# Transposes two to a bank, a second job's places sooner, and branch hints in a two-layer expert kernel

## The chip, the cores and the metric

The kernel runs on one core of one Trainium2 chip. The metric is the device time of one execution in microseconds (us); the median of three runs of the kernel before is 590.13 us (589.78 to 592.05). Profiles come from one further execution, recorded by the hardware profiler.

## The reference

Three parts follow one another, all in float32:

```
x = retention(q, k, v, lam)              # 2 x 8 heads x 768 x 64, blocks of 64 -> x: 1536 x 512
logits = x @ w_gate; noisy = logits + log1p(exp(x @ w_noise)) * noise
top2 of 8 experts per token, softmax over the two
x[token] = sum over its two experts of weight * relu(x @ w1[e]) @ w2[e]     # 512 -> 1024 -> 512
logits = x @ w_gate2; e = argmax; weight = softmax(logits)[e]
out[token] = weight * relu(x @ u1[e]) @ u2[e], for the first 384 tokens of each expert, else 0
```

## The kernel before, in words

**Matmuls.** Each float32 operand is split into two float32r parts, a high one and the rest, and a product is made of three matmuls (`three`, L954 to L956; where both parts of the tokens fit into one bank of 512 columns, two matmuls, `weighted`, L1016 and L1017). TensorE (PE) only writes to PSUM, which has eight banks; the kernel names them `hp` and `tr` (two each) and `yp0` to `yp3`.

**Jobs.** The tokens of one expert, or a part of them, are a `Job`: it gathers its rows from DRAM by an indirect DMA on GpSimd (POOL; L552), adds the two rows of each token in the second layer (`both`, L563), transposes them into columns (`split_rows`: PE transposes at L941, ScalarE (ACT) casts the high part out of the bank at L943, VectorE (DVE) subtracts it to get the rest at L946), runs the first and second product of its expert, scales and scatters its rows (`finish`, L1204 and L1206, `scatter`, L1213). A job of one tile of tokens (`by_token`) makes its hidden rows first (`first_rows`, L1064) and turns them (`turn`: transposes L1072, cast L1075, subtraction L1076). The last job of all (`ends`) writes its output in halves.

The first layer has nine jobs: 288 tokens chosen early, 128 tokens (B), and seven of 408 down to 364 tokens. The second layer has jobS (256 tokens of the fullest expert, as far as known early), jobT (up to 128 more tokens of the same expert), and seven of 336, 128, 324, 128, 164, 152 and 128 tokens. `experts` walks through the steps of each job, and inside them fetches weights (SyncE, SP, L91 and L94), converts them (`convert`, ACT L109; `convert_low`, DVE L115), prepares the next job and finishes the last one; `extra1` and `extra2` put the routing between the steps.

**Places.** `one_hot` works out for a small job which tokens it has. It multiplies a marked matrix with columns of numbers (PE, L404), copies the resulting lines from PSUM to one buffer `tabi` (DVE, L406), transposes them by PE (L409) into `a` (DVE, L410), and sums. A first call reads the token numbers; `rest` reads the others: whether the place is taken, and the weight's three parts. From these come the destinations of the scatter (`dst`, L426 and L427) and the weights (`wt`, L428). jobS calls `rest` at its successor's first step, jobT at its own second step; `finish` of jobS stands in jobT's second step, that of jobT in the step after jobT.

**Leftovers.** Tokens beyond the fixed sizes are counted, and two `tc.If(total > 0)` blocks (L1567 after layer one, L1702 after the sixth job of layer two) hold a loop for them. With these inputs the total is zero and each engine takes the branch past the block. Each engine loads the total into a register (L1294), compares and branches.

**Order.** The order of instructions on each engine is made at build time by a list scheduler: by readiness in a cost model, and earlier program text first. `tc.issue_after(ins)` keeps what is traced in its block behind `ins` on that engine's queue. Each engine then works through its queue in order, waiting at an instruction until its semaphores are there.

## Time and profile before

| | us |
|---|---|
| median of 3 runs | 590.13 |
| lowest, highest | 589.78, 592.05 |
| the profiled execution's own time | 594.88 |
| its span, first to last instruction | 593.3 |
| busy: PE, PE weight loads, DVE, ACT, POOL | 580.3, 551.6, 378.6, 278.2, 173.0 |

Matmuls are pipelined and the profile models their ends, so that PE is busy for 98% of the span does not say that it runs at its peak; gaps between the starts of its matmuls, and its waits, say more. Attention fills about the first 75 us, layer one goes to about 396 us, layer two from there.

### The profile page before, as it was taken

The page shows a single profiled execution, that of the slowest core. Times are in us where ns is not written, and L with a number is a line of the kernel's source. Part 1 is how long each engine was busy: PE and PEld are TensorE (multiplying, and loading weights), DVE is VectorE, ACT ScalarE, POOL GpSimd, SP SyncE. Part 2 cuts the span into 40 slices and gives each one's busy share as a digit, 9 for nine tenths or more (in the row PEclk, how much of TensorE's full clock was granted, in tenths as well). Part 3 has the DMA queues.
Part 4 walks back from the last instruction along what each step waited for, and adds up shares of the span by engine and source line. Part 5 has one row for each costly group of instructions (what it writes and reads, how often), then busy time and mean ns, then how long its engine had stood idle before and what let it go on. Part 6 is the DMA issues. An engine that isn't in the chain of part 4 may idle for free. (4 is left out here: it accounts for less than half of the span.)

```text
span 593.3 us, 11528 instructions
## 1 busy us (share of the span) xinstructions
PE 580.3 (98%) x4269; PEld 551.6 (93%) x4269; DVE 378.6 (64%) x878; ACT 278.2 (47%) x496; POOL 173.0 (29%) x244
## 2 busy tenths in 40 slices
PE   8999999999999999999999999999989999999996
PEld 7988899989999999999999999988879999998996
DVE  6579689865364543644645545656877667667893
ACT  4666440454353433533535334244137367467782
POOL 4966300505030040120400502023275136141304
PEclk9999999999999999999999999999999999999999
DMA  9999616349444286385443512461588967966740
GB/s 183 228 281 260 200 38 195 96 153 344 135 162 145 89 269 196 117 265 155 165 166 108 194 56 58 149 218 56 175 274 294 324 194 245 324 196 219 260 147 35
DMA packets 104483, 109.26 MB, mean 184 GB/s; under 512 B 35457, under 2 KB 80513, under 8 KB 104418
## 3 DMA queue, kind: packets, MB, share of 16 engines
q1 hardware_dynamic: 96722, 83.05, 46.4%
q0 software_dynamic: 7696, 25.39, 12.3%
q8 instruction: 35, 0.57, 0.4%
q14 instruction: 30, 0.25, 0.1%
HBM read 91.39 MB, written 18.18 MB: 185 GB/s over the span
## 5 line engine op out<-in xcount | busy, mean ns | idle before, releaser
L115 DVE TENSOR_TENSOR wl<-wst,wh 128x1024 fp32r<-128x1024 f32 x107 | 135.2, 1272 | 51.6 <-ACT wh L109 46.7
L109 ACT CAST wh<-wst 128x1024 fp32r<-128x1024 f32 x107 | 111.6, 1049 | 34.4 <-PE yp L955 26.5
L954 PE MATMUL hp<-x,wh 128*128 128x364 f32 (+9 forms) x352 | 115.9, 330 | 1.0 <-PEq L1567 1.0
L955 PE MATMUL hp<-x,wh 128*128 128x364 f32 (+9 forms) x352 | 115.6, 329 | 0.0
L956 PE MATMUL hp<-x,wl 128*128 128x364 f32 (+9 forms) x352 | 114.7, 326 | 0.0
L1043 ACT ACTIVATE h<-hp 128x364 fp32r<-128x364 f32 (+9 forms) x88 | 41.1, 467 | 154.3 <-PE hp L956 140.0
L954 PE MATMUL yp<-h,wh 128*128 128x364 f32 (+8 forms) x320 | 106.4, 333 | 0.0
L956 PE MATMUL yp<-h,wl 128*128 128x364 f32 (+8 forms) x320 | 105.9, 331 | 0.0
L955 PE MATMUL yp<-h,wh 128*128 128x364 f32 (+8 forms) x320 | 105.4, 329 | 0.0
L1044 DVE SCALAR_TENSOR_TENSOR h<-hp,h 128x364 fp32r<-128x364 f32 (+9 forms) x88 | 46.2, 525 | 60.7 <-ACT h L1043 50.1
L1213 POOL DMA_INDIRECT x<-y,Rdst x22 | 21.9, 995 | 182.0 <-DVE y L1187 179.6
L954 PEld LDWEIGHTS hp<-x,wh 128*128 128x128 f32 x352 | 66.1, 188 | 2.0 <-ACTq L1567 1.3
L955 PEld LDWEIGHTS hp<-x,wh 128*128 128x128 f32 x352 | 66.1, 188 | 0.5
L956 PEld LDWEIGHTS hp<-x,wl 128*128 128x128 f32 x352 | 66.1, 188 | 0.0
L955 PEld LDWEIGHTS yp<-h,wh 128*128 128x128 f32 x320 | 60.3, 188 | 0.5 <-issue 0.2
L956 PEld LDWEIGHTS yp<-h,wl 128*128 128x128 f32 x320 | 60.3, 188 | 0.0
L954 PEld LDWEIGHTS yp<-h,wh 128*128 128x128 f32 x320 | 60.1, 188 | 0.0
L946 DVE TENSOR_TENSOR x<-tr,x 128x128 fp32r<-128x128 f32 (+9 forms) x68 | 27.3, 430 | 22.6 <-ACT x L943 22.1
L943 ACT CAST x<-tr 128x128 fp32r<-128x128 f32 (+9 forms) x68 | 24.3, 383 | 34.9 <-PE tr L941 34.2
L563 POOL TENSOR_TENSOR xg<-xg 128x512 f32<-128x512 f32 (+1 forms) x16 | 23.5, 1473 | 38.5 <-DMA xg<-x,Tsrc 24.4
L115 DVE TENSOR_TENSOR wl<-more,wh 128x1024 fp32r<-128x1024 f32 x21 | 28.2, 1357 | 3.5 <-ACT wh L109 3.5
L552 POOL DMA_INDIRECT xg<-x,Rsrc x22 | 24.4, 1110 | 18.2 <-DVE x L946 11.8
(410 smaller groups left out, 1043.2 us busy)
## 6 DMA issues: line engine op xcount, KB each, us to landing
wst<-in_moe_w_dram SPq DMA_DIRECT2D x107, 512.0 KB
more<-in_moe_w_dram SPq DMA_DIRECT2D x21, 512.0 KB
ldk<-in_k_dram SPq DMA_DIRECT2D x12, 256.0 KB
ldv<-in_v_dram SPq DMA_DIRECT2D x12, 256.0 KB
out_dram<-zero SPq DMA_DIRECT2D x12, 256.0 KB
x<-xr SPq DMA_DIRECT2D x11, 256.0 KB
ldq<-in_q_dram SPq DMA_DIRECT2D x5, 512.0 KB
ldq<-in_q_dram SPq DMA_DIRECT2D x2, 256.0 KB
```

What stands on the lines that cost most here:

```text
L109: tail["cast"] = nc.scalar.copy(hi, st).ins
L115: tail["low"] = nc.vector.tensor_sub(lo, st, hi.bitcast(F32)).ins
L552: i = nc.gpsimd.indirect_dma_start(out=r, out_offset=None, in_=x, in_offset=bass.IndirectOffsetOnAxis(ap=src(s)[:m], axis=0))
L563: tail["both"] = nc.gpsimd.tensor_add(a, a, b).ins
L943: a = nc.scalar.copy(hi[:, d, :c], ps[:, :c])
L946: v_ = nc.vector.tensor_sub(lo[:, d, :c], ps[:, :c], hi[:, d, :c].bitcast(F32))
L954: nc.tensor.matmul(ps, a[0], b[0], start=start, stop=False)
L955: nc.tensor.matmul(ps, a[0], b[1], start=False, stop=False)
L956: tail["pe"] = nc.tensor.matmul(ps, a[1], b[0], start=False, stop=stop).ins
L1043: tail["act"] = nc.scalar.activation(hh, ps, AF.Relu).ins
L1044: tail["dve"] = nc.vector.scalar_tensor_tensor(hl, ps, 0.0, hh.bitcast(F32), op0=OP.max, op1=OP.subtract).ins
L1213: i = nc.gpsimd.indirect_dma_start(out=target, out_offset=bass.IndirectOffsetOnAxis(ap=dst, axis=0), in_=y, in_offset=None, bounds_check=t ...
```

## The change

Three things change.

**Transposes.** `split_rows` took a bank for each of the four column blocks of 128 and cast and subtracted each by itself. Now, where the tokens (rounded up to whole tiles) are at most 256, a bank takes two column blocks side by side, 256 columns each, and one cast and one subtraction handle both. This holds for eight jobs: B of layer one, and of layer two jobS, jobT, and those of 128, 128, 164, 152 and 128 tokens. Others keep one block to a bank.

**Places.** `rest` can be given a list `held`: then it leaves out the computation of `dst` (the lines up to L427, moved as they are into `places`) and appends it to the list as a function, and computes `wt` directly. jobS and jobT are both called so at step 0 of jobT, one behind the other, with the other seven jobs' weights (`later[1][7]()`) between. `finish` runs the held function first, behind the last subtraction of `turn` (`tail["h"]`) on DVE.

**Hints.** `likely` marks a branch hint for all five engines, behind the last traced instruction of each: for the first `If` at step 7 of layer one's last job, for the second at step 1 of the job of layer two ahead of it.

```diff
-        def rest(tag=tag):
+        def rest(tag=tag, held=None):
+            def places():
...
             if not whole:
                 columns(2, 6, False, tag)
...
+            if held is None:
+                places()
             else:
+                held.append(places)
             nc.vector.tensor_reduce(wt[:rows_, :nt], a[:, :, 3:6], axis=AX.X, op=OP.add)
...
     def split_rows(g, n, rows_, at=None):
...
-        for d in range(DC):
-            ps = bank("tr", [P, 512])
-            for s, m in enumerate(whole_tiles(whole, rows_)):
-                nc.tensor.transpose(ps[:, s * rows_:s * rows_ + m], g[s][:m, d * w:d * w + P], ident[:m, :m])
-            c = min(n, whole)
-            a = nc.scalar.copy(hi[:, d, :c], ps[:, :c])
+        c, k = min(n, whole), 2 if whole <= 256 else 1
+        for d in range(0, DC, k):
+            ps = bank("tr", [P, k, 512 // k])
+            for i in range(k):
+                for s, m in enumerate(whole_tiles(whole, rows_)):
+                    nc.tensor.transpose(ps[:, i, s * rows_:s * rows_ + m],
+                                        g[s][:m, (d + i) * w:(d + i) * w + P], ident[:m, :m])
+            a = nc.scalar.copy(hi[:, d:d + k, :c], ps[:, :, :c])
...
-            v_ = nc.vector.tensor_sub(lo[:, d, :c], ps[:, :c], hi[:, d, :c].bitcast(F32))
+            v_ = nc.vector.tensor_sub(lo[:, d:d + k, :c], ps[:, :, :c], hi[:, d:d + k, :c].bitcast(F32))
...
         def finish(self):
...
+            for f in self.held:
+                with tc.issue_after(tail["h"]):
+                    f()
...
+    def likely(label):
+        with ExitStack() as order:
+            for x in ("pe", "act", "dve", "pool", "sp"):
+                order.enter_context(tc.issue_after(tail[x]))
+            tc.mark_branch_hint_location(label, "LikelyTaken", ENGINES)
...
     def extra1(j, i):
...
+            if i == 7:
+                likely("over1")
...
-    with tc.If(total > 0):
+    with tc.If(total > 0, label="over1"):
...
     def extra2(j, i):
+        if j == BEFORE + 1 and i == 1:
+            likely("over2")
...
         if j == 1 and i == 0:
             with tc.issue_after(tail["pe"]):
-                jobS.rest()
+                jobS.rest(held=jobS.held)
                 later[1][7]()
+                jobT.rest(held=jobT.held)
             places.append(more[2])
         if j == 1 and i == 1:
-            with tc.issue_after(tail["pe"]):
-                jobT.rest()
...
-    with tc.If(total > 0):
+    with tc.If(total > 0, label="over2"):
```

## Rows read from the trace of the kernel before

**Rows 1.** Page, part 1: busy us (share of the span) and instructions.
```profile
PE 580.3 (98%) x4269; PEld 551.6 (93%) x4269; DVE 378.6 (64%) x878; ACT 278.2 (47%) x496; POOL 173.0 (29%) x244
```
**Rows 2.** Waits of PE, whole span: us in total, times, longest.
```profile
PE yp L409 <- DVE tabi L406: 1.5, 1, 1.5
PE yp L1109 <- ACT y L1206: 0.6, 1, 0.6
```
**Rows 3.** Timeline 436.9 to 446: start, us, instruction [idle before <-releaser].
```profile
437.16 0.83 PE L404 MATMUL yp<-ohs,aux 128*4 128x128 bf16 x12
437.82 1.17 DVE L427 TENSOR_TENSOR Sdst<-Stok,Sfar 128x2 int32<-128x2 f32 x1
437.87 0.69 ACT L1206 ACTIVATE y<-yp,Swt 128x512 f32<-128x512 f32 x1 [1.37 <-DVE Swt L428]
438.61 0.50 PE L1109 MATMUL yp<-wh,h 128*128 128x512 f32 x1 [0.61 <-ACT y L1206]
439.00 0.67 DVE L1076 TENSOR_TENSOR h<-tr,h 128x512 fp32r<-128x512 f32 x1
440.25 0.27 DVE L406 COPY tabi<-yp 4x128 f32<-4x128 f32 x1
440.58 0.22 PE L409 MATMUL yp<-iw,tabi 4*128 4x4 f32 x1 [1.47 <-DVE tabi L406]
440.73 0.50 PE L1109 MATMUL yp<-wl,h 128*128 128x512 f32 x1
442.00 1.01 PE L1072 MATMUL tr<-iw,hr 128*128 128x128 f32 x4
445.36 0.79 PE L941 MATMUL tr<-iw,xg 128*128 128x128 f32 x6
```
**Rows 4.** Windows: us, busy of PE, PEld, DVE, ACT, POOL, granted clock, DMA share, GB/s.
```profile
442.00:445.40 3.40, 3.40 (x12) 2.71 (x11) 0.69 (x1) 0.59 (x1) 0.70 (x1) 0.51 0.97 311
396.00:398.00 2.00, 0.99 (x7) 0.72 (x6) 1.30 (x5) 1.80 (x3) 0.11 (x1) 1.00 0.07 22
```
**Rows 5.** Timeline 430 to 437, some instructions of PE, DVE, ACT and POOL.
```profile
431.33 1.22 DVE L115 TENSOR_TENSOR wl<-wst,wh 128x1024 fp32r<-128x1024 f32 x1
431.49 1.47 PE L404 MATMUL tr<-oh,aux 128*4 128x256 bf16 x12
433.32 0.41 DVE L406 COPY tabi<-tr 4x256 f32<-4x256 f32 x1
433.98 2.63 DVE L115 TENSOR_TENSOR wl<-wst,wh 128x1024 fp32r<-128x1024 f32 x1 [0.25 <-ACT wh L109]
433.99 0.28 PE L409 MATMUL tr<-iw,tabi 4*128 4x4 f32 x2
435.82 3.15 POOL L563 TENSOR_TENSOR xg<-xg 128x512 f32<-128x512 f32 x2 [0.30 <-DMA xg<-x,Tsrc]
435.91 0.59 ACT L1075 CAST h<-tr 128x512 fp32r<-128x512 f32 x1 [1.96 <-PE tr L1072]
436.54 0.15 DVE L410 COPY Soa<-tr 128x8 f32<-128x8 f32 x1
```
**Rows 6.** PE's queue at the two branches (source views; ns min/median/max), and PE's timeline.
```profile
L1567 PEldq COMPARE_BRANCH  x1: 1580/1580/1580, 395.8 to 395.8; - x1
L1702 PEldq COMPARE_BRANCH  x1: 345/345/345, 537.0 to 537.0; - x1
396.36 0.33 PE L956 MATMUL yp<-h,wl 128*128 128x364 f32 x1
397.70 0.36 PE L954 MATMUL hp<-x,wh 128*128 128x256 f32 x1 [1.01 <-PEq L1567]
```
**Rows 7.** A wait over the whole span, and jobT's splitting and first matmul.
```profile
PEld tr L941 <- DVE x L946: 2.8, 12, 0.3
426.75 0.47 DVE L946 TENSOR_TENSOR x<-tr,x 128x128 fp32r<-128x128 f32 x2
428.55 0.28 PE L954 MATMUL hp<-wh,x 128*128 128x256 f32 x1
```

## The prediction

> **What bounds the kernel now.** I read the page's busy times first: PE is busy 98% of the span, every other engine far less [rows 1]. So only what makes PE wait, run slower or do more can move the end. The list of PE's waits comes next: outside the attention part and the first branch the largest is 1.5 us, for DVE's copy into `tabi`, and beside it 0.6 us for ACT's scaling of jobS's output [rows 2]. Both stand in one place of the timeline, jobT's second step [rows 3], which I read line by line, with the granted clock behind it [rows 4] and the six us before it [rows 5]. Last come the two branches [rows 6] and the splitting of a small job [rows 7]. Nowhere behind jobT does the list of PE's waits name a weight transfer, and the chain that ended last is nearly all PE; I take it that time saved at 440 us is kept to the end.

> The stall, as the reader should see it in [rows 3]: at 437.16 PE takes up jobT's twelve column matmuls (L404, 0.83). At 437.99 it wants to begin jobT's second product (L1109), whose bank `yp0` ACT has yet to empty: ACT starts at 437.87, having waited 1.37 for jobS's weights (`Swt`), and PE goes on at 438.61. After one L1109 stands the transpose L409 of jobT's line in PE's queue. Its line is copied by DVE's L406 at 440.25, because DVE has L427 (1.17), L1076 (0.67) and the scaling of jobS's second tile ahead of it. PE waits 1.47 to 440.58. [...]

> **Part by part, against the profiled execution (span 593.3, own time 594.88, 4.75 above the median of 590.13).**

> *Places sooner.* From 437.16 to 445.36, where the next job's transposes start, are 8.20 us. The work in them at full clock: the columns 0.83; L409, 440.58 to 440.73, 0.15; six L1109, of which five took 440.73 to 442.00, 1.27, so 1.5; four transposes L1072, 0.4 (an estimate from the 1.01 that they take, pipelined, at half the clock); six further matmuls of the same 512 columns, 1.5. Together 4.38. So 3.82 is lost: 0.62 + 1.72 as idle time around the one L1109 (437.99 to 438.61, and about 438.86 to 440.58), and the other 1.5 by the clock [rows 3, 4].

> After the change jobT's columns and transpose stand a step earlier, behind jobS's columns at 431.49 to 432.96 [rows 5]. They still cost PE 0.83 + 0.15, now there, so the end of the step moves from 437.16 to 438.14. ACT's L1206 no longer waits for `Swt` behind L426 and L427: jobS's line is in `a` at 436.69 (L410) and the weights are summed next, with one small instruction between, by about 437.1. ACT's L1075, moved by 0.98 with the matmuls ahead of its transposes, ends at 437.48, L1206 at 438.17. PE waits 0.03 and then has L1109, L1072 and the six others in one piece: 438.17 + 1.5 + 0.4 + 1.5 = 441.57 in place of 445.36: **3.8 us less**. It holds the return of the full clock: the idle time of 1.01 us at the first branch left the granted clock at 1.00 [rows 4, 6], and no idle time as long remains here. If the clock falls all the same, 1.5 of the 3.8 are not won.

> What the step adds is a new wait, of jobT's transpose for its line in the new place. jobT's copy needs the buffer that jobS's transposes read until about 434.2 (L409, 433.99), and in that moment DVE starts a weight subtraction, L115, which takes 2.63 in place of 1.22 [rows 5]. Queued behind the waiting transpose on PE is all of the step's second half. Two ends. If the copy goes ahead of L115, it is done by 434.6 and PE has jobT's columns and other matmuls to do until then: no wait. L115 then ends some 0.7 later, at 437.3, and L1076 at about 438.1, in time for the fifth L1109. If it goes behind L115, it is done at about 437.0 (436.54 + 0.15 + 0.27), while the scheduler, reckoning L115 at about its ordinary 1.22, has put the transpose some 1.4 us too early: PE waits up to 1.4 and the gain is 2.4. I take no wait: the copy is earlier in program text than the conversion, and DVE idled 0.25 just ahead of that L115. The held L426 and L427 of both jobs then stand behind L1076, and only the scaling of jobS's second tile (which PE does not want) and scatters come after them; I cost them at nothing, and at 1.2 for L427 if that cover were gone.

> The slow L115 lies beside POOL's additions L563 (435.82 to 438.97) [rows 5]. [...]

> *Transposes.* PE's transposes are as many as before. ACT and DVE lose two instructions each in eight jobs, on engines that do not set the end: nothing. At best the waits of PE's weight loads for a free bank go, 2.8 us in twelve over the whole span, the longest 0.3 [rows 7]; eight jobs of these could give some 1 us, but they overlap with running matmuls. At worst the first block of a job comes later by one more subtraction, about 0.25 (half of 0.47). Cover: in jobT two blocks are subtracted by 427.22, 1.33 us ahead of the first matmul at 428.55 [rows 7]; if that were gone, 8 x 0.25 = 2.0. I take 0, ends -1 and +2.0.

> *Hints.* On PE the first branch took 1.58, the second 0.345 [rows 6]. With the first like the second, the branch would be over at 396.15, before PE's last matmul ends (396.36 + 0.33), and of the 1.01 idle most would go. But DVE and ACT continue as before, and the routing behind them feeds PE again, so a lead of PE alone is partly spent waiting. Ends 0 and 1.0; I take 0.3. The second branch has nothing to give. The hints themselves, one per engine and branch, I cost at nothing behind PE's queue; at the other end each spoils the fetch of the code that follows, 1.58 - 0.345 = 1.24 each time.

> The sum: 3.8 + 0.3 = 4.1 less, a span near 589.2 in the profile, and **590.13 - 4.1 = 586.0** in the plain runs.

> **Rivals.**

> *The line behind the weights.* The transpose waits up to 1.4 as worked out: 2.4 + 0.3 = 2.7, **587.4**. For it: L115 starts in the very moment in which jobS's transposes end. Against it: DVE's idle 0.25.

> *Slower: the stall moves and grows.* If jobT's transpose is queued on PE right behind its columns, at about 433.8 (432.96 + 0.83), while the copy comes behind L115 at 437.0, PE idles 3.2 instead of 2.3. Then the clock falls again, and what now runs from 432.96 to 437.16, 4.2 us of matmuls, comes behind the wait: 437.0 + 4.2 + 1.7 (half of 3.4 us at half clock) + 3.4 for the rest is 446.3 against 445.36. With no gain at the branch: **591.0**. It decides if the transpose stands more than about 2.5 us ahead of the copy's end. Against it: for jobS the scheduler left 1.0 us of other matmuls between the columns and their transpose, 432.96 to 433.99 [rows 5].

> *The hints cost a fetch.* Code ahead of a branch or behind it is fetched too late because the hinted block took its place: twice 1.24, so 586.3 + 2.5 = **588.8**, without the branch's 0.3. Against it: nothing in these rows shows a hint. [...]

> *The plain runs have less of the stall.* The profiled execution is 4.75 above their median; part of the stall and the fall of the clock may belong to that. Then some 1 us of 4.1 is won: **589.1**.

> **How the numbers follow.** The forecast 0.50, the line behind the weights 0.17, the slower one 0.08, the fetch 0.10, the plain runs 0.15. About 0.5% (3 us: below 587.2 or above 593.1) can be told from no change. The forecast's own range is 584.5 to 587.2 (clock kept, branch 0 to 1.0, transposes to -1). Faster takes 0.47 of its 0.50, 0.09 of the second and 0.04 of the last two: 0.60. Slower by 3 us needs the slower rival together with the transposes' +2.0 or the fetch: 0.04. Same: 0.36. The range 584.3 to 590.4 leaves out the slower rival and little at either end.

> **What would show it.** Right: the columns of jobT (L404, twelve) directly behind jobS's and no PE wait for `tabi`; L1109 six in a row; a granted clock of 1.00 from 430 to 455; casts of 128x256 and 128x512 in `split_rows` at no new wait of PE; PE's first branch nearer 0.35. Wrong: a wait of over 1 us of PE for `tabi` at 434 to 437, a granted clock below 1 there, or gaps of PE at the starts of the small jobs.

## The result, and the profile after

The kernel after takes 596.18 us (median of 6 runs, 594.53 to 597.73) against 591.31 of the kernel before measured beside it (589.78 to 592.47): a ratio of 1.0085, 95% interval 1.0068 to 1.0102, slower by some 5 us. Measured once more, in a later group of runs (E12 below), it was 1.0060 (1.0041 to 1.0078). The prediction was 586.0 with a range of 584.3 to 590.4, and gave "slower" 0.04.

The profiled execution of the kernel after took 597.44, its span is 595.8. The lines of the kernel after are some ten higher than those of before (`three` is L963 to L965, the columns L405, `tabi` L407, jobs' output scaling L1219, the branches L1588 and L1724). PE's waits behind 380 us, which answer to [rows 2] (us in total, times, longest; PEq is PE's sequencer):

```profile
PE yp L964 <- PEq L1588: 2.4, 1, 2.4
PE yp L963 <- ACT h L1053: 2.3, 1, 2.3
PE tr L410 <- DVE tabi L407: 0.5, 1, 0.5
PE yp L965 <- PEq L1724: 0.3, 1, 0.3
```

The wait of 1.5 for `tabi` has become 0.5, and the 0.6 for `yp` is gone. In their place stand two larger ones: 2.4 at the first branch (1.01 before, [rows 6]) and a new one of 2.3 for ACT's `h`. The stretch that answers to [rows 3] (timeline: start, us, instruction, idle time before it and its releaser):

```profile
436.30 0.83 PE L405 MATMUL yp<-ohs,aux 128*4 128x128 bf16 x12
437.94 0.28 PE L410 MATMUL tr<-iw,tabi 4*128 4x4 f32 x2 [0.49 <-DVE tabi L407]
438.79 0.22 PE L410 MATMUL yp<-iw,tabi 4*128 4x4 f32 x1
440.59 0.50 PE L1119 MATMUL yp<-wh,h 128*128 128x512 f32 x1
440.93 0.40 PE L1119 MATMUL yp<-wl,h 128*128 128x512 f32 x1
441.17 0.39 PE L1119 MATMUL yp<-wh,h 128*128 128x512 f32 x1
441.40 0.40 PE L1119 MATMUL yp<-wl,h 128*128 128x512 f32 x1
441.64 0.62 PE L1119 MATMUL yp<-wh,h 128*128 128x512 f32 x2
442.10 0.60 PE L1082 MATMUL tr<-iw,hr 128*128 128x128 f32 x4
```

This is what the first step of the prediction said: jobT's columns and transpose stand a step earlier, and the six matmuls L1119 run without a gap. The wait of 0.49 is for jobS's line. DVE's copies of both lines, at 437.48 and 438.19, come behind a weight subtraction that takes 2.30, beside POOL's addition:

```profile
435.20 1.27 POOL L570 TENSOR_TENSOR xg<-xg 128x512 f32<-128x512 f32 x1
435.26 2.30 DVE L116 TENSOR_TENSOR wl<-wst,wh 128x1024 fp32r<-128x1024 f32 x1
437.48 0.41 DVE L407 COPY tabi<-tr 4x256 f32<-4x256 f32 x1
```

So the order is that of the rival "the line behind the weights", at 0.49 in place of up to 1.4. The loss comes a few us later. ACT's timeline there, and PE's:

```profile
446.91 2.00 ACT L110 CAST wh<-wst 128x1024 fp32r<-128x1024 f32 x2
453.11 0.69 ACT L1219 ACTIVATE y<-yp,Dwt 128x512 f32<-128x512 f32 x1 [4.20 <-issue]
453.70 0.44 ACT L1053 ACTIVATE h<-hp 128x336 fp32r<-128x336 f32 x1
```

```profile
451.58 0.32 PE L965 MATMUL hp<-x,wl 128*128 128x336 f32 x1
454.19 0.42 PE L963 MATMUL yp<-h,wh 128*128 128x336 f32 x1 [2.30 <-ACT h L1053]
```

ACT stands still for 4.20 us ahead of jobT's output scaling, and "issue" says that nothing which the profile shows held it back. Queued behind it is the `h` that PE wants for the next job, of 336 tokens. PE runs out of work for 2.30 us and then, from 455.2 to 458.6, runs at a granted clock of 0.50. The windows, which answer to [rows 4] (us, busy of PE, PEld, DVE, ACT, POOL, granted clock, DMA share, GB/s):

```profile
442.00:445.40 3.40, 3.40 (x22) 2.72 (x20) 1.41 (x5) 1.37 (x3) 1.81 (x2) 1.00 0.98 315
455.20:458.60 3.40, 3.40 (x14) 3.40 (x13) 3.40 (x4) 3.05 (x4) 2.86 (x3) 0.50 0.83 309
```

At 442 the granted clock is now 1.00, and the same 3.4 us at half clock (0.51 before, 0.50 here) have moved to 455. The branches (source views; ns min/median/max), and PE's timeline at the first, answer to [rows 6]:

```profile
L1588 PEldq COMPARE_BRANCH  x1: 4152/4152/4152, 394.3 to 394.3; - x1
L1724 PEldq COMPARE_BRANCH  x1: 363/363/363, 538.8 to 538.8; - x1
396.03 0.33 PE L963 MATMUL yp<-h,wh 128*128 128x364 f32 x1
398.77 0.40 PE L964 MATMUL yp<-h,wh 128*128 128x364 f32 x1 [2.41 <-PEq L1588]
```

PE's first branch did not fall from 1.58 towards 0.35, it rose to 4.15. The two profiles add up: the 3.82 of the stall gone less 0.49 that is left of it, 1.40 more at the branch (2.41 less 1.01), 2.30 behind ACT's stop and 1.7 for the 3.4 us at half clock, together +2.1 of the 2.5 by which the spans differ. That the plain runs differ by 5 is a second matter: the profiled execution of before lies 3.6 above the median of the six runs beside it, that of the kernel after 1.3 above its own (see E11 and E15).

### The profile page after: what moved, and what is told of

The parts are those of the page before. It is cut to its first block, busy times and chain, and to the rows that moved or that the text cites. A ratio compares the mean times of both kernels' runs of the same rounds, so it can differ in the third digit from the quotient of the medians.

```text
span 595.8 us, 11507 instructions
## 1 busy us (share of the span) xinstructions
PE 580.4 (97%) x4269; PEld 553.0 (93%) x4269; DVE 374.2 (63%) x862; ACT 276.2 (46%) x480; POOL 174.5 (29%) x244
## 5 line engine op out<-in xcount | busy, mean ns | idle before, releaser
L116 DVE TENSOR_TENSOR wl<-wst,wh 128x1024 fp32r<-128x1024 f32 x107 | 132.1, 1243 | 53.4 <-ACT wh L110 50.8
L963 PE MATMUL hp<-x,wh 128*128 128x364 f32 (+9 forms) x352 | 115.9, 330 | 0.0
L965 PE MATMUL hp<-x,wl 128*128 128x364 f32 (+9 forms) x352 | 114.9, 327 | 0.0
L963 PE MATMUL yp<-h,wh 128*128 128x364 f32 (+8 forms) x320 | 106.8, 334 | 2.3 <-ACT h L1053 2.3
L965 PE MATMUL yp<-h,wl 128*128 128x364 f32 (+8 forms) x320 | 106.1, 332 | 0.0
L963 PEld LDWEIGHTS hp<-x,wh 128*128 128x128 f32 x352 | 66.4, 189 | 0.7 <-issue 0.2
L965 PEld LDWEIGHTS hp<-x,wl 128*128 128x128 f32 x352 | 66.3, 188 | 0.0
L963 PEld LDWEIGHTS yp<-h,wh 128*128 128x128 f32 x320 | 60.4, 189 | 2.6 <-ACT h L1053 2.6
L965 PEld LDWEIGHTS yp<-h,wl 128*128 128x128 f32 x320 | 60.6, 189 | 0.0
L955 DVE TENSOR_TENSOR x<-tr,x 128x384 fp32r<-128x384 f32 (+9 forms) x52 | 25.1, 515 | 22.1 <-ACT x L952 22.0
L570 POOL TENSOR_TENSOR xg<-xg 128x512 f32<-128x512 f32 (+1 forms) x16 | 26.1, 1635 | 40.1 <-DMA xg<-x,Tsrc 26.8
L952 ACT CAST x<-tr 128x384 fp32r<-128x384 f32 (+9 forms) x52 | 22.0, 452 | 32.2 <-PE tr L950 31.7
L116 DVE TENSOR_TENSOR wl<-more,wh 128x1024 fp32r<-128x1024 f32 x21 | 29.4, 1410 | 3.5 <-ACT wh L110 3.5
L559 POOL DMA_INDIRECT xg<-x,Rsrc x22 | 26.1, 1188 | 18.2 <-DVE yT L516 11.8
```

Of the source, the lines that this page charges most:

```text
L116: tail["low"] = nc.vector.tensor_sub(lo, st, hi.bitcast(F32)).ins
L559: i = nc.gpsimd.indirect_dma_start(out=r, out_offset=None, in_=x, in_offset=bass.IndirectOffsetOnAxis(ap=src(s)[:m], axis=0))
L570: tail["both"] = nc.gpsimd.tensor_add(a, a, b).ins
L952: a = nc.scalar.copy(hi[:, d:d + k, :c], ps[:, :, :c])
L955: v_ = nc.vector.tensor_sub(lo[:, d:d + k, :c], ps[:, :, :c], hi[:, d:d + k, :c].bitcast(F32))
L963: nc.tensor.matmul(ps, a[0], b[0], start=start, stop=False)
```

## The experiments

Each ratio is to the kernel before, run beside it in the same group of runs on the same chip, with its 95% interval. Before took 590.6 in the group of E1 to E4, 594.2 in that of E5 to E8, 590.4 in that of E9 to E12 and 590.8 in that of E13 to E16; why the second is slower is not known, and the record gives the same chip number for it as for the last. "Branch" is the time of PE's first branch. "Packets" counts the 8 KB packets of instruction code in the DMA view of queue q14 (30 packets, 0.25 MB on the pages of before and after; q8 has 35 of 16 KB, 0.57 MB), from 5 us before to 6 us behind POOL's first branch. No view names the engine that a packet is for; the author took those of q8 for PE's and those of q14 for the other engines'. "Stop" is ACT's idle time ahead of jobT's scaling (L1219; L1206 in before).

| | kernel | ratio | branch, us | packets | stop, us |
|---|---|---|---|---|---|
| | before, its three profiles | | 1.58, 1.96, 2.16 | 2, 2, 2 | none |
| | after | 1.0085 (1.0068 to 1.0102) | 4.15 | 1 | 4.2 |
| E1 | no hints | 0.9990 (0.9973 to 1.0008) | 4.36 | 2 | none |
| E2 | no pairs | 0.9987 (0.9972 to 1.0003) | 2.17 | 2 | none |
| E3 | old places | 1.0053 (1.0034 to 1.0072) | 3.71 | 1 | 2.7 |
| E4 | code padded behind the branch | 1.0066 (1.0049 to 1.0084) | 3.73 | 1 | elsewhere |
| E5 | hints, not ACT's | 0.9972 (0.9948 to 0.9995) | 4.64 | 2 | none |
| E6 | ACT's hints alone | 1.0065 (1.0043 to 1.0087) | 3.78 | 1 | 3.6 |
| E7 | places alone | 0.9965 (0.9941 to 0.9990) | 1.80 | 2 | none |
| E8 | no hints, last job single | 0.9969 (0.9944 to 0.9994) | 1.76 | 2 | none |
| E9 | six ACT instructions ahead | 1.0039 (1.0018 to 1.0059) | 4.30 | 2 | none |
| E10 | first hints sooner | 1.0084 (1.0058 to 1.0111) | 3.53 | 1 | 3.2 |
| E11 | before again | 1.0005 (0.9989 to 1.0022) | 1.96 | 2 | none |
| E12 | after again | 1.0060 (1.0041 to 1.0078) | 3.23 | 1 | 3.5 |
| E13 | ACT's second hint alone left | 0.9999 (0.9989 to 1.0009) | 3.65 | 2 | none |
| E14 | ACT's first hint alone left | 1.0055 (1.0040 to 1.0071) | 4.29 | 1 | 4.4 |
| E15 | before a third time | 0.9993 (0.9978 to 1.0009) | 2.16 | 2 | none |
| E16 | E8 once more | 0.9982 (0.9966 to 0.9997) | 2.74 | 2 | none |

**E1, no hints.**

```diff
-            if i == 7:
-                likely("over1")
-        if j == BEFORE + 1 and i == 1:
-            likely("over2")
```

> The kernel after without its two branch hints, all else kept. Theory A (code): ACT's 4.2 us gap ahead of the output scaling of job T and PE's long first branch (4.15 us) come from code that has to be fetched behind a taken branch; the hints fetch nothing for PE. Then the gap stays within an instruction or two of its place, PE's branch still takes about 4 us, and the time stays within 1 us of the kernel after (595 to 597). Theory B (hints): the hints themselves put the fetch at a bad time. Then PE's first branch takes 1.6 us again, the ACT gap is gone, and the time is 3 us or more below the kernel after (593 or less).

Measured: 590.42 (588.62 to 592.40). Half of each theory held. ACT's stop is gone with the hints, and with it the loss against before; PE's branch, which theory B wanted short, still took 4.36. So the two new waits have two causes.

**E2, no pairs.**

```diff
-        c, k = min(n, whole), 2 if whole <= 256 else 1
+        c, k = min(n, whole), 1
```

> The kernel after with one column block to a bank again (the sixteen casts and sixteen subtractions are back). Theory A (code): ACT has some thirteen instructions more ahead of the same place, so the place where it waits for code lies in an earlier step, where PE has other work or waits anyway, and PE's first branch stands behind the last job's matmuls again and takes about 1.6 us: 4 to 6 us below the kernel after, 589 to 592. Theory C (places): the 2.6 us wait of PE at 451.6 comes from the earlier places and the order of the queues behind them: the time stays within 1.5 us of the kernel after.

Measured: 590.22 (589.19 to 591.61), PE's branch 2.17, no stop. As theory A had it, and yet the hints are in this kernel: they do harm only together with the pairs.

**E3, old places.**

```diff
-                jobS.rest(held=jobS.held)
+                jobS.rest()
                 later[1][7]()
-                jobT.rest(held=jobT.held)
...
         if j == 1 and i == 1:
+            with tc.issue_after(tail["pe"]):
+                jobT.rest()
```

> The kernel after with the old order of the places of jobs S and T. Theory A (code): the stall at 437 to 441 us is back (3 us more than in the kernel after) and ACT's gap ahead of job T's output scaling stays, since no ACT instruction has moved: 597 to 600. Theory C (places): the gap at 451.6 goes with the earlier places: PE waits at 437 to 441 as before, not at 451, and the time is 2 us or more below the kernel after (594 or less).

Measured: 594.03 (592.35 to 596.03). The stop stays (2.7 us), so the earlier places did not make it: theory C falls. The 3 us that theory A added for the old stall did not come; PE's two waits for `tabi` were 0.9 and 0.7 and the clock did not fall there.

**E4, ACT's code padded behind the branch.** Fifteen copies in the body of the first `If`, which is jumped over.

```diff
     with tc.If(total > 0, label="over1"):
...
+        for _ in range(15):
+            nc.scalar.copy(spare, spare)
```

> The kernel after with fifteen copies of one column on ACT inside the first branch's body, which is skipped in this run: no instruction more is executed on ACT, only its code behind the branch lies fifteen instructions further on. Theory A (code): ACT's 4 us gap comes fifteen instructions sooner in its order, at 434.7 to 439.3 us, where ACT idles 4.6 us anyway; PE's wait of 2.6 us at 451.6 and the half clock behind it (3.4 us) go, PE's first branch stays at 4 us: 3.5 to 5 us below the kernel after, 591 to 593. Theory C or any theory by data: nothing that is executed differs, so the gap and the time stay (595 to 597).

Measured: 594.52 (593.50 to 595.99), ratio 1.0066. The kernel after had 1.0085 and, in E12, 1.0060, so no gain can be told, where 3.5 us or more were expected. ACT executes the same instructions, and its stop ahead of L1219 is gone, which no theory by data allows. But a stop is found elsewhere (ACT's waits, 425 to 570 us), at 558.2 us, behind the second branch, and PE feels it there:

```profile
ACT wh L110 <- issue: 2.0, 1, 2.0
```

```profile
PE hp L1026 <- DVE hr L1037: 1.3, 1, 1.3
```

So fifteen instructions that are not executed took away the stop at 449 (4.2 us, and 3.5 in E12), and one of 2.0 stands at 558; that its place goes with where the code lies is the author's reading of this. The wait of 1.3 does not account for the 3.9 us by which E4 lies above before; the rest is open.

**E5 and E6, hints by engine.**

```diff
-ENGINES = (ET.PE, ET.Activation, ET.DVE, ET.Pool, ET.SP)
+ENGINES = (ET.PE, ET.DVE, ET.Pool, ET.SP)      # E5
+ENGINES = (ET.Activation,)                     # E6
```

> The kernel after with the hints of PE, DVE, POOL and SP kept and those of ACT left out. Theory D (ACT's hint): ACT's stop ahead of job T's output scaling comes from its own hint, behind which the code past the branch's target is no longer fetched ahead. Then the stop of 4.2 us is gone, PE has no wait at 451, PE's first branch stays at about 4 us, and the time is that of the kernel without hints (590 to 591.5). Rival E (any hint): the fetches of the other engines' hints hold up ACT's. Then the stop stays and the time is 594 or more.

> The kernel after with ACT's two hints alone. Theory D (ACT's hint): the stop of 3 to 4 us ahead of job T's output scaling is there and PE waits 1 to 2.5 us at 451 with the half clock behind it: 594 to 597. Rival E (any hint): with one engine's hints the stop is gone, 590 to 592.

Measured side by side: 593.00 (591.36 to 595.71) without ACT's hints, 597.53 (595.24 to 599.22) with ACT's alone, before at 594.17. The times of all kernels are higher in this group, so the ratios decide: 0.9972 and 1.0065. The hints of the other four engines are harmless, ACT's own cost 0.9%, which is 5.5 us. Theory D holds over rival E.

**E7, places alone** (E1 and E2 together).

> The kernel before with the earlier places alone: no hints, one column block to a bank. From the prediction's step (the stall at 437 to 441 us goes, 3.8 us): 586 to 588. From the chip so far (without pairs but with hints the kernel took 590.2 against 590.6 before, though its profile shows the stall gone): the plain runs of before have less of this stall than its profiled run, 588.5 to 590.5. PE's first branch takes 1.6 to 2.2 us in both.

Measured: 592.00 (590.20 to 594.09), 0.35% below before: 2.1 us, with an interval of 0.6 to 3.5. Not the 3.8 of the prediction's step.

**E8, no hints, and the last job single.** The job of 256 tokens whose transposes stand right ahead of the first branch (jobS) has one column block to a bank again.

```diff
-        c, k = min(n, whole), 2 if whole <= 256 else 1
+        c, k = min(n, whole), 2 if whole < 256 else 1
```

> The kernel after without hints, and with one column block to a bank in the one job of 256 tokens whose transposes stand right ahead of the first branch. Theory F (order at the branch): PE's first branch is long because the paired transposes let PE's sequencer come to the branch earlier, with fewer matmuls left to cover the code's fetch. Then the branch takes 1.6 to 2.2 us again instead of 4.4, PE's idle time there falls from 2.8 to 1.2 to 1.8 us, and the time is 1 to 1.5 us below the kernel without hints (589 to 589.5). Rival G (the number of instructions before the branch decides what is fetched, not the order): the branch stays at about 4 us, 590 to 591.

Measured: 592.08 (589.40 to 595.97), ratio 0.9969 against E1's 0.9990; the intervals overlap. PE's branch fell from 4.36 to 1.76 and the idle time there from 2.6 to 1.2, by the one job that stands ahead of it, as theory F had it; that the whole kernel gains by it can't be told from these runs. The branch in E1 and in E8:

```profile
L1586 PEldq COMPARE_BRANCH  x1: 4360/4360/4360, 392.6 to 392.6; - x1
```

```profile
L1586 PEldq COMPARE_BRANCH  x1: 1760/1760/1760, 395.2 to 395.2; - x1
```

The other small jobs keep their pairs here, and the ratio is that of E7: pairs elsewhere neither win nor lose more than the intervals, of some 0.25% to either side.

**E9 and E10, where the hint stands against ACT's code.**

```diff
             if i == 7:
                 likely("over1")
+            if i == 1:                             # E9
+                for _ in range(6):
+                    nc.scalar.copy(spare, spare)
```

```diff
-            if i == 7:                             # E10
+            if i == 5:
                 likely("over1")
```

> The kernel after with six copies of one column on ACT some fifteen us ahead of the first branch: six instructions are executed more (under 1 us of an engine that waits there anyway), and all of ACT's code behind lies six instructions further on. Theory H (meeting): ACT's next 8 KB of code are asked for at a fixed place of its code; in the kernel after this place comes about half a microsecond before the hint, two us before such a fetch lands, and the hint takes its place, so the code behind the branch's target is missing later. With six instructions ahead that place is passed some six us before the hint, as in the kernel without pairs: a second fetch shows around 390 us, ACT's stop of 4 us is gone, and the time is 3 to 5.5 us below the kernel after. Rival D (the hint alone): whatever stands ahead of it, the code behind the target is not fetched ahead, and the stop only moves by six instructions: within 1.5 us of the kernel after.

> The kernel after with the first branch's hints two steps of the expert sooner on all engines. Theory H (meeting): ACT's hint then lies ahead of the place where its next code is asked for, which happens undisturbed some 8 us later: no stop, 3 to 5.5 us below the kernel after. Rival D (the hint alone): the stop stays, within 1.5 us of the kernel after. For PE: if its hint fetched anything, a 16 KB fetch would follow the hint here and PE's first branch would fall from 4 us to under 2; if it fetches nothing the branch stays at 3.7 to 4.6 us.

Measured: E9 593.16 (591.27 to 595.14), E10 594.51 (592.38 to 597.03), E12 beside them 593.67. E9's time, expected 3 to 5.5 below the kernel after, is 0.5 below. By the profiles each theory lost one. With six instructions ahead the stop is gone and there are two packets, the first at 390.3 us, five us ahead of the hint (395.1): against rival D. With the hint at 382.3, a dozen us ahead of the branch, the stop of 3.2 us stays and there is one packet: against the "meeting" of theory H. What fits both, and the packets of every row of the table, is an order of hint and packet. With pairs and without ACT's hint (E1, E5, E13) there are two packets, and the second starts 1.1 us behind ACT's branch; the hint of the kernel after stands 0.8 us ahead of that branch (394.75 and 395.59), and there is one. In E2 and E9 the packet comes 5.9 and 4.8 us ahead of the hint, and there are two. That ACT's next 8 KB are asked for at a fixed place of its code, and that a hint ahead of this place takes the packet away, is the author's inference; no view shows a request. The DMA view of the kernel after, of E1 and of E9, in the same stretch:

```profile
q14 instruction: 1, 0.01, 0.2%
```

```profile
q14 instruction: 2, 0.02, 0.4%
```

```profile
q14 instruction: 2, 0.02, 0.4%
```

A packet comes late: in all six profiles with a stop ahead of L1219, and in E4's stop at 558.2, one packet of q14 starts inside the stop, and ACT goes on 1.16 to 1.21 us behind its end. In the kernel after this packet starts at 451.60 and takes 0.31, and ACT goes on at 453.11 (DMA view, 451.5 to 452.0):

```profile
q14 instruction: 1, 0.01, 3.9%
```

In PE the sooner hint (381.1) is followed by no 16 KB packet of q8 until 393.8, and its branch took 3.53: nothing shows a fetch by PE's hint. Open is the time of E9. With no stop it still lies 2.8 us above before. Its profile accounts for that at the branch: 2.5 us of idle time there, and behind it

```profile
399.20:402.60 3.40, 3.31 (x15) 3.34 (x16) 0.28 (x1) 1.16 (x3) 0.11 (x1) 0.50 0.02 5
```

3.4 us at half clock (the eighth number is the granted clock). Such a stretch right behind the first branch is in 5 of the 11 profiles in which the pairs stand ahead of it (E3, E5, E6, E9, E14) and in none of the 7 in which they don't; why one execution has it and the next not was not settled.

**E11 and E15, the kernel before again**, with no edit.

> The kernel before once more, unchanged. If its profiled run of 594.9 us was a run with more of the stall than usual, this profile shows a shorter wait for the table at 437 to 441 us and an own time nearer to 590.6; if the stall is the same in every run, the wait is 1.3 to 1.8 us with the half clock of 3.4 us behind it again, and what the profiled run had more lies in the first 385 us.

> The kernel before a third time, for its profile. If the stall at 437 to 441 us on which the prediction rested is an accident of one execution (DVE's weight subtraction beside POOL's sums), it is absent or under 0.5 us again; if the second profile was the exception, PE waits 1 us or more for the table here.

Measured: 590.33 (589.59 to 593.46) and 590.18 (588.28 to 593.41); the profiled executions took 589.96 and 589.77, not 594.88. In neither is there a wait for `tabi` among PE's waits behind the attention part. E11's timeline, which answers to [rows 3, 5]:

```profile
432.54 2.38 POOL L563 TENSOR_TENSOR xg<-xg 128x512 f32<-128x512 f32 x1 [0.29 <-DMA xg<-x,Tsrc]
432.58 1.20 DVE L115 TENSOR_TENSOR wl<-wst,wh 128x1024 fp32r<-128x1024 f32 x1
435.00 0.15 DVE L427 TENSOR_TENSOR Sdst<-Stok,Sfar 128x2 int32<-128x2 f32 x1
436.82 0.50 PE L1109 MATMUL yp<-wh,h 128*128 128x512 f32 x1
436.92 0.28 DVE L406 COPY tabi<-yp 4x128 f32<-4x128 f32 x1
437.26 0.22 PE L409 MATMUL yp<-iw,tabi 4*128 4x4 f32 x1
437.41 0.51 PE L1109 MATMUL yp<-wl,h 128*128 128x512 f32 x1
```

The weight subtraction that took 2.63 in the first profile takes 1.20 (1.20 in E15), L427 takes 0.15 in place of 1.17, and `tabi` is ready before PE asks. The stall on which the prediction rested is in one of three profiles of before. What differs is which engine is slowed: here POOL's addition takes 2.38, where it took 1.30 beside the slow subtraction. Over all 18 profiles this subtraction took 1.83 to 2.63 in twelve, with POOL's addition at 1.27 to 1.42, and 1.20 to 1.23 in six, with the addition at 1.98 to 2.50. How many plain runs have the stall is not known, in the slower group of E5 to E8 least of all, where no profile of before was taken.

**E12, the kernel after again.**

> The kernel after once more, unchanged, on the same chip as the others of this call. If ACT's stop belongs to the code and not to chance, it stands again ahead of job T's output scaling, 2.5 to 4.5 us long, and the time is 0.6 to 1.1 per cent above the kernel before.

Measured: 593.67 (591.87 to 594.78), the stop 3.5 us long in its old place, PE's wait 1.6: it belongs to the kernel, not to one execution. Here and in E6 the list of waits names POOL's addition L570 as what ACT's L1219 waited for; in E13 L1219 starts at 446.38, before that addition (446.82), so it is not what L1219 needs.

**E13 and E14, ACT's hints by branch.** `ALL` is short for the five engines, `NOT_ACT` for the four others.

```diff
+ENGINES = {"over1": NOT_ACT, "over2": ALL}     # E13
+ENGINES = {"over1": ALL, "over2": NOT_ACT}     # E14
-            tc.mark_branch_hint_location(label, "LikelyTaken", ENGINES)
+            tc.mark_branch_hint_location(label, "LikelyTaken", ENGINES[label])
```

> The kernel after with ACT's hint for the first branch left out; ACT's hint for the second branch and all hints of the other engines stay. Theory I (a hint stops the sequential fetch): the hint, given before ACT's next block of code has been asked for, takes the place of that fetch; only the first branch's hint leads to a stop that PE feels (the one ahead of job T's scaling). Then the stop is gone and the time is that without ACT's hints, 0.997 to 1.001 of before. Rival J (both branches' hints cost): half or more of the loss stays, 1.003 or more, with a stop of ACT behind 540 us.

> The kernel after with ACT's hint for the second branch left out, all else kept. Theory I (a hint stops the sequential fetch): the stop of 3 to 4 us ahead of job T's output scaling is there, PE waits 1.3 to 2.5 us behind it, and the time is that of the kernel after, 1.005 to 1.009 of before. Rival J (both branches' hints cost): 1.001 to 1.004.

Measured: 590.68 (590.10 to 591.80) and 594.56 (593.12 to 596.33). The one instruction, ACT's hint for the first branch, is worth 0.56% here, 3.3 us (0.93% between E5 and E6; the intervals overlap). E13's L1219 starts without a stop:

```profile
446.38 0.69 ACT L1219 ACTIVATE y<-yp,Dwt 128x512 f32<-128x512 f32 x1
```

E14's waits of ACT and of PE, and its clock behind the branch and behind the stop:

```profile
ACT y L1219 <- issue: 4.4, 1, 4.4
```

```profile
PE yp L964 <- PEq L1588: 2.5, 1, 2.5
PE yp L963 <- ACT h L1053: 2.5, 1, 2.5
```

```profile
395.70:399.10 3.40, 2.98 (x13) 3.01 (x14) 0.62 (x1) 1.19 (x3) 0.11 (x1) 0.50 0.02 5
453.70:457.10 3.40, 3.40 (x12) 3.40 (x13) 3.04 (x4) 3.40 (x5) 2.14 (x3) 0.51 0.92 356
```

Both of the change's faults are there, each with 3.4 us at half clock behind it.

**E16, the best version again** (E8, in a group of runs where before takes 590.8).

> The fastest of the variants again, on another chip: earlier places, pairs in the jobs of under 256 tokens, no hints. If what it won over before (0.3 per cent) is real on a chip where before takes some 590.4, it is 0.995 to 0.998 again; if that gain came from runs of before with the stall in them, 0.999 to 1.001.

Measured: 589.18 (588.22 to 591.34), 0.18% below before with an interval of 0.03 to 0.34: about 1 us, between the two ranges expected. PE's branch took 2.74 here, 2.2 of it idle, so what the single job wins there varies. The version beats both kernels, before by little.

## Why the prediction was wrong

Two terms of the sum failed: "places sooner" took its 3.8 from a stall that two of three profiles of before don't have, and "hints" was put at 0.3 won where ACT's hint cost 3.3 to 5.5 us. A third, "transposes", put at 0, made the first branch of PE longer.

*What bounds the kernel* was read rightly: PE's waits set the time. But the list of waits is of one execution. Its own time, 594.88, lay 4.75 above the median, and the largest wait on it outside the attention part was treated as the kernel's. The rival "the plain runs have less of the stall" says just this and had 0.15; E11 and E15, without the stall, speak for its premise.

*Places sooner, 3.8.* The mechanism was right in the execution that it was read from: the columns a step earlier, L1119 in one row, a granted clock of 1.00 at 442, 0.49 of new wait for `tabi`, for jobS's line and not jobT's, where 0 was taken and up to 1.4 allowed for. One row was misread: in [rows 3, 5] `Swt` waits for L426 alone, since L428, which sums it (437.69), stands ahead of L427 (437.82); the sum does not change by it. The size was wrong for ordinary runs: 2.1 us alone in E7 (0.6 to 3.5), in the group where before was slow, and about 1 us in E16, with pairs in the other jobs.

*Transposes, 0.* Right for the jobs in general (E8 against E7), wrong for the one job whose transposes stand ahead of the branch. The working looked for waits on banks and casts and did not ask where in PE's order the branch would come to stand. In the built order of the kernel before the column blocks of jobS lie between the last job's matmuls; with pairs they go in one run, and two of that job's matmuls have slipped behind the branch. PE's sequencer is at the branch at 394.30 where it was at 395.81, and the 16 KB packet of q8 starts at 395.98 where it started at 395.05 ahead of the branch. So the branch begins earlier and ends later, at 398.45 in place of 397.39. In eleven profiles with pairs there it took 3.2 to 4.6 us, in seven without 1.6 to 2.7. In all 18 profiles PE's branch ends 1.3 to 1.5 us behind the end of such a packet; the packet starts 0.9 to 2.2 us behind the branch's start with pairs there, and from 0.8 ahead of it to 0.3 behind it without. That jobS's pairs make the branch long is shown by E8; that they do it through the order and the time of the packet is argued from the timelines and the packets, and why the packet itself comes later is not shown.

*Hints, 0.3 won.* This step failed in sign. PE's hint bought nothing (E6, without it: 3.78; E10, sooner: 3.53). The cost at the other end, 1.24 twice, was priced as a longer branch. ACT's own branch had nothing to win: it takes 0.07 us with the hint and 0.05 without. What went with the hint is one of two packets of q14, and ACT stops 54 us behind the hint, at 448.91, and for 4.2 us. How much of the 3.3 to 5.5 us goes through this stop is not shown, since E9 has the hint and no stop and still lies 2.8 us above before. The rival "the hints cost a fetch" came nearest, with the wrong place and size, at 588.8 and with 0.10. That a hinted block takes the place of other code, as it had it, is shown by no run; the runs show one packet in place of two and, 53 to 64 us behind the hint, the stop.

*The clock returns at 442*: right, at 1.00 granted. It fell to 0.50 at 455 in its stead, behind a wait of 2.3.

*The chance.* "Slower" got 0.04 because each rival was priced alone and against the whole of the forecast gain. Where the stall is missing, as in two of three profiles of before, little was left to set against two losses, one of them at a place where ACT has no stop in the three profiles of before.

What stays open: that the missing packet is ACT's own is inferred, though closely (in all 18 profiles there is one packet with ACT's hint ahead of the packet's place and two without, and each stop ends 1.16 to 1.21 us behind a late one). How a hint comes to leave a packet out is not shown: in E1, E5 and E13 the packet starts only behind ACT's branch, by 1.1 us. The times of E9 and E4 are open too.

## What to carry to other kernels

Before a gain is read from one wait in one profile, see how far the profiled execution lies above the median; if that is as much as the wait, take a second profile of the same kernel, since the wait may be the difference. ACT's hint went here with one packet of code in place of two and a stop of up to 4.4 us, those of the other four engines with neither (E5): when a hint or a branch changes, read the packets of code and the stops engine by engine, and look for a stop with a late packet inside it, far behind the branch (53 to 64 us here) as well as at it. The name alone does not tell: two of the six stops bore POOL's name, and the 4.05 us of "issue" ahead of L1075 in the first profile of before end with PE's transposes (442.00 and 1.01). And an edit that reorders PE's work ahead of a branch is not to be priced at nothing there: here the branch took 3.2 to 4.6 us with the pairs ahead of it, 1.6 to 2.7 without.
